# Output products in column tiles of 384 and 256 + 128 tokens, and two products of a unit in swapped order

## The chip, the cores and the metric

The kernel runs on one core of a Trainium2 chip. The metric is the device time of one launch in microseconds (us); lower is better. Before the change the median of three runs was 2621.24 us (2618.13 to 2623.8).

## What is computed

All in fp32: a causal convolution of seven taps (softmaxed per head, 8 heads) over 8 sequences of 4096 tokens with 192 features, and then on the 32768 tokens a feed-forward block with RMS norm and SwiGLU, width 1536.

```python
w = softmax(weight, axis=-1)                        # 8 heads x 7 taps
x = conv(x_pad, w)                                  # (8, 4096, 192) -> (32768, 192)
xn = x / sqrt(mean(x * x) + 1e-6) * rms_g
g, val = xn @ w_gate, xn @ w_val                    # 192 -> 1536
out = (silu(g) * val) @ w_out                       # 1536 -> 192
```

## The kernel before

**Tiling.** The tokens are worked off in 32 pairs; a pair is two groups (g = 0, 1) of T = 512 tokens. The first pair goes through a plain routine (lines 991 and 1031). The other 31 each go through one `Pair` object, and these are nearly the whole time. One such pair is 60 products and then 42 output steps, on the matmul engine in the order of `Pair.products`.

**Products (line 754).** The hidden layer is computed in four units. A unit makes six tiles of 128 hidden features by 512 tokens (three feature blocks for two token groups), once for the gate and once for the value. By a fast matrix scheme it needs 15 products in place of 18; the right-hand sides are sums of token tiles (`XSUM`, tile `xc`, made by VectorE and GpSimd), the left-hand sides sums of weight blocks (`WSUM`). Every product is two matmuls of 64 rows by 512 columns that run side by side: h = 0 (gate) on the lower half of the array's rows, h = 1 (value) on the upper half. `CHAIN` and `CHAINS` give their order as (unit, bank v, index of the product): (0, 4, 5) adds product 5 into the PSUM bank that stands for v = 4. The kernel before already swaps two products of unit 0, so its unit 0 begins (4,11), (1,4), (5,6), (4,9), (0,8), (4,5), (5,13), (1,10), (4,7), (0,3), (5,2), (2,1).

**Evacuations.** Between the products of one bank its value is copied or added up by ScalarE (A), VectorE (V) or GpSimd (G). `Unit.do` has the steps: `S41` copies bank 4 after its second product into a tile (line 706 on ScalarE, 710 on VectorE), `S42` the same after its third; `S00` copies bank 0; `C` adds bank 5 to the tile copied by `S40` (line 774); `D5` adds the tile of `S00` into bank 5 (line 770); `S51` copies bank 5 after that; `F2` copies bank 4 into a new bank 2; `R` makes a result (line 778). The second figure is h. A product that adds to a bank must wait until the copy of the bank's former value is done.

**Order of the other engines.** `ORDER` is a list written by hand. `p2` stands for two entries of the matmul stream, and each other word for one step: the engine's letter, the step, v, h and the unit; a trailing `-` means a step of the pair before. Engines run in order, so the list sets the order within each engine; between engines only waits on data count. Further steps of the list: `VT11`, `VT21` turn output banks by 32x32 transposes (line 899), `Vbc` is one small transpose for the norm (line 490) that waits for two copies on GpSimd (line 483), `Gmul` scales by the norm (line 498), `Dst0`, `Dst1` store an output group (line 957), `Dload` loads tokens (line 144), `Dplace` and `DfetA`, `DfetB` move normed tokens to device memory and back as tiles (lines 633, 659). All `D` steps are issued by SyncE, except a part of the last pair's stores by ScalarE.

**Output steps (line 884).** The output product is a seven-product scheme over token groups, pairs of feature blocks and the two halves of the 192 outputs: `OUTS` lists the forms, 42 steps in all. A step multiplies one tile of 128 features by 512 tokens with a weight block of three times 32 columns (m = 0, 1, 2). The array is used as four column tiles of 32 columns (i = 0 to 3), each with its own weights and its own stream of tokens, writing its own 32 partitions of the same PSUM bank, 384 columns in use. Before the change the step is eight matmuls: four of 256 tokens (m = 0 on tiles 0 and 1, m = 1 on tiles 2 and 3, each tile taking every other block of 32 tokens) and four of 128 tokens (m = 2, a quarter of the tokens each). In fp32 every matmul shows in the trace as two records (two passes), each with its own weight load.

Of the kernel before, what the change touches and what calls it, by code (L numbers as in the profile page):

```python
# [19 lines left out]
def kernel(  # L20
# [11 lines left out]
    P = nc.NUM_PARTITIONS  # L32
# [10 lines left out]
    T = 512  # L43
# [3 lines left out]
    HP = P // 2  # L47
    KP = D // HP
    Q = 32
    NQ = P // Q  # L50
# [7 lines left out]
    LOW, UPP = slice(0, HP), slice(HP, P)  # L58
# [29 lines left out]

    SPAN = 1509
    ORDER = (  # L90
        "p2 VT11- p2 AS40.1.0 AS40.0.0 p2 AF0.0.0 GX9- AF0.1.0 Dst0- p2 VC.1.0 Dload- GX4- p2",
        "Vbc- AS41.0.0 VS41.1.0 VC.0.0 p1 AS00.1.0 p1 Gmul- VT21- AS00.0.0 p2 AS42.0.0",
        "VS42.1.0 p2 VD5.0.0 p1 VD5.1.0 AS51.0.0 p1 Dst1- VR1.0.0 AS51.1.0 p2 VR1.1.0 AF2.0.0",
        "p2 AF2.1.0 VR0.0.0 Dplace- AG1.0.0 p1 VR0.1.0 p1 AF3.0.0 AF3.1.0 p2 VR2.0.0 AG0.0.0",
        "p1 VR2.1.0 p1 AS44.0.0 GM0.1.0 AS44.1.0 p2 VR3.0.0 AG2.0.0 GM1.1.0 p1 VR3.1.0 p1",
        "AS40.0.1 VR5.0.0 AS40.1.1 p2 AG4.0.0 VR5.1.0 AG5.0.0 p1 VM4.1.0 p1 AF0.0.1 VF0.1.1",
# [140 lines left out]
    def load_out(i):  # L237
# [28 lines left out]
        out=taps[:], in0=w_sb[:], in1=stat[:].to_broadcast([P, H, K]), op=ALU.subtract  # L266
# [7 lines left out]
        out=taps[:], in0=taps[:], in1=ssum[:].to_broadcast([P, H, K]), op=ALU.mult  # L274
# [153 lines left out]
    def part_tap(p, k, j):  # L428
# [4 lines left out]
        if k == 0:  # L433
            h = SIDE[j]
            acc[p, j] = h, pick(h, False)
# [11 lines left out]
        if k == K - 1:  # L447
            h, i = acc.pop((p, j))
            free[h].append(i)
            ended[p] = ended.get(p, 0) + 1  # L450
            if ended[p] == len(SIDE):
                x_sb.pop(p)
# [229 lines left out]
    def pick(h, full):  # L682

        i = next((i for i in free[h] if ((h, i) in whole) == full), free[h][0])
        free[h].remove(i)
        return i
# [5 lines left out]
    def put(at, do):  # L692
        heapq.heappush(line, (at, next(tick), do))
# [10 lines left out]
    def copy(eng, dst, src, s=1):  # L704
        if eng == "A":
            nc.scalar.activation(out=dst, in_=src, func=AF.Copy, scale=float(s))  # L706
        elif s < 0:
            nc.vector.tensor_scalar(out=dst, in0=src, scalar1=-1.0, scalar2=None, op0=ALU.mult)
        else:
            nc.vector.tensor_copy(out=dst, in_=src)  # L710
# [5 lines left out]
    CHAINS = [  # L716
        [(u, 4, 11)] + [(u - 1, 4, 0)] * (u > 0) + [(u, *c) for c in CHAIN] for u in range(NU)
    ]
    CHAINS[0][2:4] = CHAINS[0][3:1:-1]
    CHAINS[-1][-3:] = [(NU - 1, 4, 12), (NU - 1, 2, 1), (NU - 1, 3, 14), (NU - 1, 4, 0)]  # L720
    FORK = {0: (1, 1), 2: (4, 1), 3: (5, -1)}
    RESULT = {1: ("42", -1), 0: ("41", -1), 2: ("51", -1), 5: ("44", -1), 3: ("c", 1)}
# [83 lines left out]
    NM = D // (2 * Q)  # L806
# [13 lines left out]
    )  # L820
    HOME = {"X": 0, "Y": 1, "Z": 1}
    SIDE = (0, 1, 0)
    RIGHT = {1: B11, 2: B21, 3: B22, 4: T4, 5: T1, 6: T2, 7: T3}

    class Pair:
# [36 lines left out]
        def products(self):  # L862
            for u, v, i in itertools.chain(*CHAINS):
                for h in range(2):
                    self.units[u].product(h, v, i)
                    yield
            for form, b, lo, hi in OUTS:
                first = form in (1, 7)
                if first:
                    self.open(b, False)  # L870
                for k in range(lo, hi):
                    src, right = self.left(form, k), RIGHT[form][:, k]
                    fresh = first and k == 0
                    wide = src.rearrange("p (b q e) -> p q b e", q=2, e=Q)
                    slim = src.rearrange("p (b q e) -> p q b e", q=NQ, e=Q)
                    for i in range(NQ):
                        self.tile(b, i, 0, 2 * P, right[:, i // 2], wide[:, i % 2], fresh)
                    yield
                    for i in range(NQ):
                        self.tile(b, i, 2 * P, P, right[:, 2], slim[:, i], False)  # L880
                    yield

        def tile(self, b, i, at, n, left, cols, fresh):
# [30 lines left out]
        def do(self, eng, name):  # L914
            act, *at = name.split(".")
            p, n = self.p, NM * P
            if name in self.past:
                return
            self.past.add(name)
            if len(at) == 2:  # L920
                self.units[int(at[1])].do(eng, act, int(at[0]))
            elif at:
                self.sum(int(act[1]), int(at[0]), eng)
            elif act == "c1":
                self.open("Y", True)
                copy(eng, self.some("Y"), self.some("X"))
            elif act in ("s7", "c2"):
                t = self.tl[act] = tiles.pop(0)
                copy(eng, t[:, 0:n], self.some("Z" if act == "s7" else "X"))
            elif act in ("C22", "C21"):  # L930
                t = self.tl["s7" if act == "C22" else "c2"][:, 0:n]
                b = "X" if act == "C22" else "Z"
                nc.vector.tensor_tensor(out=t, in0=self.some(b), in1=t, op=ALU.add)
                if b == "Z":
                    self.close(b)
                    if p == PAIRS - 1:
                        for name in ("T22", "T21", "st1"):
                            if name not in self.past:
                                self.do(eng, name)
            elif act in ("T22", "T21"):  # L940
                t = self.tl.pop("s7" if act == "T22" else "c2")
                self.turn(t, 1, int(act[2]) - 1)
                tiles.append(t)
            elif act in ("T11", "T12"):
                b = "Y" if act == "T11" else "X"
                self.turn(self.bank(b), 0, int(act[2]) - 1)
                self.close(b)
            elif act in ("st0", "st1"):
                g = int(act[2])
                r = p * PT + g * T  # L950
                o = self.o_sb.pop(g)[:].rearrange("p a d -> p (a d)")
                o = o.rearrange("p (b d) -> p b d", d=HP)
                for c, rows, lo, hi in ((0, LOW, 0, 8), (1, UPP, 0, 8), (2, slice(0, P), 8, 12)):
                    n = T // (hi - lo)
                    to = out[r : r + T, c * HP : (c + 1) * HP].rearrange("(b p) d -> p b d", p=n)
                    q = nc.scalar if c == 1 and p == PAIRS - 1 else nc.sync
                    q.dma_start(out=to, in_=o[rows, lo:hi, :])
            else:
                self.ahead(eng, act)

# [16 lines left out]
    def plain(hts):  # L977


        groups = [(u, g, f) for u in range(NU) for g in (1, 0) for f in range(NF)]  # L980
        groups[0 : 2 * NF] = [(0, g, f) for f in range(NF) for g in (1, 0)]
        held = {}

        def products():
            for u, g, f in groups:
                if len(hts) <= u:
                    hts.append(big.tile([P, 2, NF, T], F32, name="ht"))
                bks = held[u, g, f] = [free[h].pop(0) for h in range(2)]
                for k in range(KP):
                    for h in range(2):  # L990
                        nc.tensor.matmul(  # L991
                            out=bank(h, bks[h])[:], lhsT=wf[u][HALF[h], k * NF + f, :],
                            rhs=xb[HALF[h], g, k, :], start=(k == 0), stop=(k == KP - 1),
                            skip_group_check=True,
                        )
                yield

        def silus():
            for i in groups:
                sg = tiles.pop(0)  # L1000
                nc.scalar.activation(out=sg[:], in_=bank(0, held[i][0])[:], func=AF.Silu)
                held[i].append(sg)
                yield

        def values():
            for u, g, f in groups:
                *bks, sg = held.pop((u, g, f))
                nc.vector.tensor_tensor(  # L1008
                    out=hts[u][:, g, f, :], in0=bank(1, bks[1])[:], in1=sg[:], op=ALU.mult
                )  # L1010
                tiles.append(sg)
                for h in range(2):
                    free[h].append(bks[h])
                yield

        return products(), silus(), values()

    LAG = 138
# [114 lines left out]
    p, sl, v = plain(hts)  # L1133
# [31 lines left out]
    c = base + 200  # L1165
# [4 lines left out]

    for j in range(len(SIDE)):
        put(c + 240 + 700 * (j // 2), functools.partial(part_tap, 2, 0, j))
        for k in range(1, K):
            at = c + 250 + 100 * k + 50 * j if j < 2 else c + 960 + 80 * k
# [58 lines left out]
```

## Time and profile before

The profiled execution took 2620.28 us, of which the span of the profile is 2618.4 us.

| Item | Value |
|---|---|
| median of 3 runs | 2621.24 us |
| profiled execution / its span | 2620.28 us / 2618.4 us |
| matmul records, weight loads | 29002 each |
| busy: VectorE / ScalarE / GpSimd | 2265.0 / 1617.3 / 2079.0 us |
| one pair, the commonest length | 79.5 us: 52.06 us of products, 27.44 us of output steps |
| first pair and set-up, to the first product of line 754 | 136.76 us |

A pair's length is the distance between the starts of the first product matmul (line 754) of one pair and of the next. In the page, PE is the matmul stream and PEld the weight loads beside it. A busy matmul engine need not be at its peak, since matmuls overlap: the distance between the starts of matmuls on the same tile says more than the length of one.

### The profile page before, as it was taken

To read this page: it belongs to the slowest core of one execution; us is meant where nothing else is said; L and a number is where in the kernel's file an instruction comes from. 1 tells how busy PE (TensorE), PEld (TensorE's weight loads), DVE (VectorE), ACT (ScalarE), POOL (GpSimd) and SP (SyncE) were. 2 spreads that over 40 slices of the span, in tenths; PEclk is the share of its full clock that TensorE was granted. 3 is DMA by queue.
4 is the path that set the end of the run, shared out by engine and by line. 5 is a ranking of instruction groups with operands and counts; after the bars stand their busy time and mean duration, and the time that the engine had idled before them with its cause. 6 is when DMAs were issued, how large, how long until landed. Compare 5 with 4: busy or idle time off the path is not lost.

```text
span 2618.4 us, 71028 instructions
## 1 busy us (share of the span) xinstructions
PE 2580.3 (99%) x29002; PEld 1866.1 (71%) x29002; DVE 2265.0 (87%) x3617; ACT 1617.3 (62%) x2967; POOL 2079.0 (79%) x1693
## 2 busy tenths in 40 slices
PE   6999999999999999999999999999999999999999
PEld 3677777777767777777776777777777777777776
DVE  8888888888888988888888888888898888888875
ACT  5375556765556765557755567655577555676554
POOL 3877788877888777888787887778887778877776
PEclk9999999999999999999999999999999999999999
DMA  6322331323312223213233222233132332222210
GB/s 143 54 47 51 63 53 36 63 39 63 63 36 53 50 51 63 54 35 63 39 63 63 41 48 51 51 63 58 34 59 44 58 63 43 46 57 45 50 38 14
DMA packets 510659, 138.01 MB, mean 53 GB/s; under 512 B 482300, under 2 KB 484860, under 8 KB 510205
## 3 DMA queue, kind: packets, MB, share of 16 engines
q1 hardware_dynamic: 508716, 133.18, 27.2%
q8 instruction: 227, 3.72, 0.6%
q14 instruction: 100, 0.82, 0.1%
q10 hardware_dynamic: 1616, 0.29, 0.1%
HBM read 83.87 MB, written 49.55 MB: 51 GB/s over the span
## 4 chain that ended last, share of the span: by engine, by line
PE 96%; DVE 2%; DMA 1%; issue 0%; POOL 0%; ACT 0%; SPq 0%; DVEq 0%; POOLq 0%; ACTq 0%
PE ps L754 62%; PE ps L884 33%; PE ps L991 1%; PE ps L1031 1%; DMA x<-in_x_dram 0%; DMA xb<-xd 0%; DVE y L405 0%; DVE ht L1008 0%; DVE y L420 0%; DVE y L393 0%; DVE xc L304 0%; PE ps L594 0%; DVE wf L319 0%; ACT xb L614 0%; DVE xc L668 0%
## 5 line engine op out<-in xcount | busy, mean ns | idle before, releaser
L754 PE MATMUL ps<-xc,wf 64*128 64x512 f32 x4960 | 1252.8, 592 | 1.6 <-DVE xc L668 1.1
L754 PEld LDWEIGHTS ps<-xc,wf 64*128 64x128 f32 x4960 | 760.9, 186 | 308.1 <-issue 88.8
L754 PE MATMUL ps<-xb,wf 64*128 64x512 f32 x2480 | 709.1, 589 | 0.0
L706 ACT ACTIVATE tls<-ps 128x512 f32<-128x512 f32 (+1 forms) x636 | 365.7, 589 | 375.5 <-PE ps L884 211.0
L798 POOL TENSOR_TENSOR ht<-ht,tile 128x512 f32<-128x512 f32 x295 | 375.2, 1279 | 272.8 <-ACT tile L791 271.4
L706 ACT ACTIVATE tile<-ps 128x512 f32<-128x512 f32 x697 | 400.1, 594 | 271.2 <-PE ps L754 158.4
L754 PEld LDWEIGHTS ps<-xb,wf 64*128 64x128 f32 x2480 | 392.9, 187 | 141.2 <-issue 38.7
L706 ACT ACTIVATE ps<-ps 128x512 f32<-128x512 f32 (+1 forms) x651 | 366.9, 578 | 54.1 <-PE ps L884 38.9
L912 POOL TENSOR_TENSOR early<-ht 128x512 f32<-128x512 f32 x279 | 379.2, 1364 | 4.9
L444 DVE SCALAR_TENSOR_TENSOR ps<-xh,tp,ps 128x512 f32<-128x512 f32 x450 | 312.1, 745 | 1.7 <-ACT ps L436 0.6
L798 POOL TENSOR_TENSOR ht<-ht,tls 128x512 f32<-128x512 f32 x201 | 255.2, 1276 | 72.4 <-ACT tls L791 70.9
L884 PE MATMUL ps<-ht,wo_sb 128*32 128x256 f32 (+1 forms) x6944 | 310.5, 326 | 0.0
L778 DVE TENSOR_TENSOR tile<-ps,tile 128x512 f32<-128x512 f32 x373 | 255.0, 687 | 56.1 <-PE ps L754 53.5
L884 PEld LDWEIGHTS ps<-ht,wo_sb 128*32 128x32 f32 x6944 | 216.3, 110 | 92.8 <-POOL ht L798 23.5
L884 PE MATMUL ps<-ht,x 128*32 128x256 f32 (+1 forms) x5952 | 250.1, 326 | 0.4 <-issue 0.4
L912 POOL TENSOR_TENSOR ht<-ht 128x512 f32<-128x512 f32 x186 | 248.3, 1350 | 0.0
L791 ACT ACTIVATE tile<-tile 128x512 f32<-128x512 f32 x373 | 233.1, 629 | 12.3 <-DVE tile L778 12.3
L884 PEld LDWEIGHTS ps<-ht,x 128*32 128x32 f32 x5952 | 190.5, 110 | 54.2 <-issue 1.6
L778 DVE TENSOR_TENSOR ht<-ps,tls 128x512 f32<-128x512 f32 x311 | 211.8, 681 | 0.0
L778 DVE TENSOR_TENSOR ht<-ps,tile 128x512 f32<-128x512 f32 x309 | 210.4, 681 | 0.1
L778 DVE TENSOR_TENSOR tls<-ps,tls 128x512 f32<-128x512 f32 x247 | 169.4, 686 | 28.1 <-PE ps L754 26.1
L884 PE MATMUL ps<-early,x 128*32 128x256 f32 (+1 forms) x4464 | 193.5, 326 | 0.0
(129 smaller groups left out, 3132.8 us busy)
## 6 DMA issues: line engine op xcount, KB each, us to landing
xb<-xd SPq DMA_DIRECT2D x124, 384.0 KB
xd<-yn SPq DMA_DIRECT2D x248, 96.0 KB
out_dram<-o_sb SPq DMA_DIRECT2D x184, 128.0 KB
xh<-in_x_dram SPq DMA_DIRECT2D x192, 105.0 KB
xh<-in_x_dram SPq DMA_DIRECT2D x56, 98.4 KB
ht<-in_moe_w_gate_dram SPq DMA_DIRECT2D x12, 192.0 KB
ht<-in_moe_w_val_dram SPq DMA_DIRECT2D x12, 192.0 KB
tls<-in_moe_w_out_dram SPq DMA_DIRECT2D x8, 192.0 KB
```

Source lines behind the costliest of these rows:

```text
L444: nc.vector.scalar_tensor_tensor(out=dst, in0=xk, scalar=w, in1=at, op0=ALU.mult, op1=ALU.add)
L706: nc.scalar.activation(out=dst, in_=src, func=AF.Copy, scale=float(s))
L754: nc.tensor.matmul(out=self.new(v, h, True) if first else self.old(v, h), lhsT=wf[self.u][HALF[h], WAT[i], :], rhs=x_op(XOP[i])[HALF[h]], ...
L778: nc.vector.tensor_tensor(out=self.hv(v) if h else t[:], in0=self.old(v, h), in1=t[:], op=plus(s))
L791: nc.scalar.activation(out=t[:], in_=src[:], func=AF.Silu)
L798: engine[eng].tensor_tensor(out=self.hv(v), in0=src, in1=t[:], op=ALU.mult)
L884: nc.tensor.matmul(out=self.bank(b)[i * Q : (i + 1) * Q, at : at + n], lhsT=left, rhs=cols, start=fresh, stop=True, skip_group_check=True, ...
L912: engine[eng].tensor_tensor(out=dst, in0=a, in1=b, op=op)
L991: nc.tensor.matmul(out=bank(h, bks[h])[:], lhsT=wf[u][HALF[h], k * NF + f, :], rhs=xb[HALF[h], g, k, :], start=(k == 0), stop=(k == KP - 1 ...
L1031: nc.tensor.matmul(out=bank(h, bks[h])[:, w : w + D], lhsT=hts[f // NF][HALF[h], g, f % NF, j * P : (j + 1) * P], rhs=wo_sb[HALF[h], f, :] ...
```

## The change

The output step becomes six matmuls: m = 0 and m = 1 on tiles 0 and 1, each over the first 384 tokens; m = 2 on tiles 2 and 3, over 256 tokens each; then the last 128 tokens of m = 0 and m = 1 on tiles 2 and 3. Each tile still takes 384 columns in all. The generator yields after the first four and after the last two, so a step is still two entries of the stream.

The output rows lie differently in the bank, so a store of 512 tokens becomes five DMAs in place of three (32 x 12, 32 x 12, 64 x 8, 32 x 4 and 32 x 4 rows of 64 floats, in place of 64 x 8, 64 x 8 and 128 x 4); the bytes and the rows are the same. In the last pair ScalarE issues two of the five per store, in place of one of three.

In unit 0 the products (5,13) and (4,5) change places. In `ORDER` the step `Vbc-` goes ahead of both `VC` steps, `VC.0.0` ahead of `VS41.1.0`, `AS00.0.0` and `AS00.1.0` change places, `VD5.0.0` goes ahead of `AS42.0.0` and `VS42.1.0`, and `VD5.1.0` and `AS51.0.0` keep their place after `VS42.1.0`.

```diff
     ORDER = (
-        "p2 VT11- p2 AS40.1.0 AS40.0.0 p2 AF0.0.0 GX9- AF0.1.0 Dst0- p2 VC.1.0 Dload- GX4- p2",
-        "Vbc- AS41.0.0 VS41.1.0 VC.0.0 p1 AS00.1.0 p1 Gmul- VT21- AS00.0.0 p2 AS42.0.0",
-        "VS42.1.0 p2 VD5.0.0 p1 VD5.1.0 AS51.0.0 p1 Dst1- VR1.0.0 AS51.1.0 p2 VR1.1.0 AF2.0.0",
+        "p2 VT11- p2 AS40.1.0 AS40.0.0 p2 Vbc- AF0.0.0 GX9- AF0.1.0 Dst0- p2 VC.1.0 Dload- GX4- VC.0.0 p2",
+        "AS41.0.0 VS41.1.0 p1 AS00.0.0 p1 Gmul- VT21- AS00.1.0 p2 VD5.0.0 AS42.0.0",
+        "VS42.1.0 p2 VD5.1.0 AS51.0.0 p2 Dst1- VR1.0.0 AS51.1.0 p2 VR1.1.0 AF2.0.0",
...
     CHAINS[0][2:4] = CHAINS[0][3:1:-1]
+    CHAINS[0][5:7] = CHAINS[0][6:4:-1]
...
+    WIDE = NM * P
...
-                    wide = src.rearrange("p (b q e) -> p q b e", q=2, e=Q)
-                    slim = src.rearrange("p (b q e) -> p q b e", q=NQ, e=Q)
-                    for i in range(NQ):
-                        self.tile(b, i, 0, 2 * P, right[:, i // 2], wide[:, i % 2], fresh)
+                    two = src.rearrange("p (b q e) -> p q b e", q=2, e=Q)
+                    for i in range(2):
+                        self.tile(b, i, 0, WIDE, right[:, i], src[:, 0:WIDE], fresh)
+                    for i in range(2):
+                        self.tile(b, 2 + i, 0, T // 2, right[:, 2], two[:, i], fresh)
                     yield
-                    for i in range(NQ):
-                        self.tile(b, i, 2 * P, P, right[:, 2], slim[:, i], False)
+                    for i in range(2):
+                        self.tile(b, 2 + i, T // 2, T - WIDE, right[:, i], src[:, WIDE:T], False)
                     yield
...
-                for c, rows, lo, hi in ((0, LOW, 0, 8), (1, UPP, 0, 8), (2, slice(0, P), 8, 12)):
-                    n = T // (hi - lo)
-                    to = out[r : r + T, c * HP : (c + 1) * HP].rearrange("(b p) d -> p b d", p=n)
+                wide, half = WIDE // Q, T // HP
+                for c, i, m, lo, hi, at in (
+                    (0, 0, 1, 0, wide, 0), (1, 1, 1, 0, wide, 0), (2, 2, 2, 0, half, 0),
+                    (0, 2, 1, half, wide, WIDE), (1, 3, 1, half, wide, WIDE),
+                ):
+                    n = m * Q
+                    rows = slice(r + at, r + at + (hi - lo) * n)
+                    to = out[rows, c * HP : (c + 1) * HP].rearrange("(b p) d -> p b d", p=n)
                     q = nc.scalar if c == 1 and p == PAIRS - 1 else nc.sync
-                    q.dma_start(out=to, in_=o[rows, lo:hi, :])
+                    q.dma_start(out=to, in_=o[i * Q : i * Q + n, lo:hi, :])
```

## The prediction

> **What bounds the kernel now.** I read the page first, then the waits, the chain and the timeline of an ordinary pair, and at last the starts of single matmul records.
>
> ```profile
> PE 2580.3 (99%) x29002; PEld 1866.1 (71%) x29002; DVE 2265.0 (87%) x3617; ACT 1617.3 (62%) x2967; POOL 2079.0 (79%) x1693
> ...
> q8 instruction: 227, 3.72, 0.6%
> ...
> PE 96%; DVE 2%; DMA 1%; issue 0%; POOL 0%; ACT 0%; SPq 0%; DVEq 0%; POOLq 0%; ACTq 0%
> PE ps L754 62%; PE ps L884 33%; PE ps L991 1%; PE ps L1031 1%; DMA x<-in_x_dram 0%; DMA xb<-xd 0%; DVE y L405 0%; DVE ht L1008 0%; DVE y L420 0%; DVE y L393 0%; DVE xc L304 0%; PE ps L594 0%; DVE wf L319 0%; ACT xb L614 0%; DVE xc L668 0%
> ```
>
> The matmul stream is the end-setting chain: 62% products, 33% output steps. So an edit counts only by what it does to this stream's pace or gaps. The pace of the output steps, from the timeline:
>
> ```profile
> 1003.00 7.98 PE L884 MATMUL ps<-ht,x 128*32 128x256 f32 x192
> 1010.80 1.48 PE L884 MATMUL ps<-ht,wo_sb 128*32 128x256 f32 x32
> ```
>
> 192 records at 16 per step are 12 steps, in 1010.80 - 1003.00 = 7.80 us: 650 ns a step. On one column tile the records start 216, 216, 109 and 109 ns apart. Two equations (256 and 128 columns) give 0.83 ns a column and pass, and about 2.5 ns for each record. The gaps, from the waits of PE and of its weight loads, and from the chain:
>
> ```profile
> PE ps L884 <- issue: 3.3, 5, 1.4
> ```
>
> ```profile
> PEld ps L884 <- issue: 6.1, 9, 1.6
> ...
> PEld ps L754 <- POOL xc L668: 13.4, 17, 1.0
> ```
>
> ```profile
> 1068.90 13.33 PE ps L884 x321
> 1082.23 0.53 issue
> 1082.76 14.51 PE ps L884 x264
> ```
>
> "Issue" means that no data was late; these stops lie in the output steps only. The third view shows one. And the waits in unit 0, in the timeline of a pair that starts at 1176.69 us:
>
> ```profile
> 1180.47 0.69 DVE L710 COPY tls<-ps 128x512 f32<-128x512 f32 x1
> ...
> 1180.49 0.60 ACT L706 ACTIVATE tile<-ps 128x512 f32<-128x512 f32 x1 [0.56 <-PE ps L754]
> ...
> 1181.08 0.68 DVE L774 TENSOR_TENSOR tile<-ps,tile 128x512 f32<-128x512 f32 x1
> ...
> 1181.20 0.33 PEld L754 LDWEIGHTS ps<-xc,wf 64*128 64x128 f32 x4 [0.77 <-POOL xc L668]
> ```
>
> The load at 1181.20 is that of (4,5). It names GpSimd, but GpSimd was done earlier; the copies of bank 4 (lines 706 and 710, S41) end at 1181.09 and 1181.16, and they hold it.
>
> [...] in the output steps that begin at 430.67 us one tile falls 425 ns behind after a stop, and the others' 128-column records start before its earlier 256-column ones, at an unchanged 650 ns a step and at unchanged record lengths (379 and 273 ns). [...] I see 90 ns from the last product to the first output step. [...] 227 packets of 16,384 bytes are 58,112 instructions, PE's matmuls and loads being 58,004.
>
> **Part 1, fewer records.** A step has 12 records and 12 loads for 16 and 16. It is not faster for it: tiles 2 and 3 still run 256, 256, 128 and 128 columns, 650 ns; tiles 0 and 1 run 384 twice, 2 x (320 + 2.5) = 645 ns, and wait for nothing but cannot end the step. Value taken: 0. That tiles of unequal length don't hold each other up is argued from the skewed stretch; the trace has no unequal step. Bounds: 42 x 31 = 1302 steps by -10 ns (the pure columns) = -13 us, and by +24 ns (a late load lengthened records there from 379 to 403) = +31 us.
>
> **Part 2, instruction blocks.** PE eats 32 instructions in 650 ns, 20.3 ns each; afterwards 24, 27.1 ns each. Following q8 against PE's position: a block is asked for when 0.69 of the former is eaten; PE stops when the new one has not landed by 1.54 to 1.66, about 0.97 x 256 = 248 instructions or 5.0 us later. Landing takes 1.7 us in the median, but behind the xb transfers 5.0 to 6.1 us five times, and those are exactly the long stops. Adding what each pair's output steps lost to them (pairs 4, 5, 12, 18, 19, 23 to 26: 0.56, 1.11, 0.93, 0.99, 0.82, 0.29, 0.25, 0.18, 1.97) gives 7.1 us. Afterwards there are 248 x 27.1 = 6.7 us, more than the worst landing. I take -6.8, keeping 0.3 for a worse phase; bounds 0 and -7.1.
>
> **Part 3, unit 0.** Times in us from the pair's first product; half h = 1 ends the products, so it counts. Before: 104 ns at the first product (stays), at (4,5) 141 + 105 = 246 ns, at (2,1) 116 ns, together 466. The 105 is a load that could not be hidden: the first record takes 693 instead of 589 ns.
> After: (5,13) is due at 4.40 and needs both C. VectorE: Vbc (0.24) moves to the idle time 1.38 to 2.92, its GpSimd copies being done at 1.61; C.1 2.99 to 3.68; C.0 3.60 to 4.28. Semaphore to load took 42 ns here, the second half's load follows 36 ns later: 4.37, lag 36 ns before the matmul, so about 105 - 36 = 69 ns lost. S41.1 now ends at 4.89; (4,5), due at 5.3, doesn't wait. But S42 now has one product of cover, (1,10), where it had two. (4,5) ends at 6.186; semaphore 0.18, copy 6.39 to 7.08 (0.692; VectorE is free, D5.0 ends at 6.26), load at 7.136, matmul due at 7.044: 93 + 104 = 197 ns lost at (4,7). So the old wait returns three products later. Behind it: D5.1 6.99 to 7.68, R1.0 to 8.26, R1.1 to 8.87 (9.08 before), F2.1 to 9.5; (2,1) is due at 9.81, so its 116 go. After: 104 + 69 + 197 = 370; gain 96 ns, x 30 pairs (the first waits for other things) = -2.9 us. Bounds: both new waits vanish, 362 x 30 = -10.9; nothing gained, 0.
>
> **Part 4, stores.** Two more DMAs per store on SyncE. Its cost per issue and its slack:
>
> ```profile
> 1188.38 2.02 SPq L957 DMA_DIRECT2D out_dram<-o_sb  x3
> 1190.50 5.25 SPq L633 DMA_DIRECT2D xd<-yn  x8
> 1228.70 1.29 SPq L659 DMA_DIRECT2D xb<-xd  x2
> ```
>
> 0.66 us each, four more a pair: loads (line 144) 1.3 us later, the xd writes 2.6 us later. SyncE idles from 1195.75 to 1228.70, and the loads' first readers (ScalarE, from 1228.7) come 40 us after them: cost 0. Without that cover the fetches, and the sums behind them, would be 2.6 us late. At the end nothing covers: each queue issues one more, up to 0.6 us, but the last is a quarter of the former's rows and data landed from 2614.6 to 2617.2 at a steady rate: +0.2 taken, bounds 0 and +0.6.
>
> **Sum.** -6.8 - 2.9 + 0.2 = -9.5 against the profiled execution's 2620.28 (span 2618.4 and 1.9 around it): 2610.8. The median of the runs is 1.0 above that execution: 2611.7.
>
> **Rivals.** (a) Stops stay: something other than instruction rate decides the landings. For: two stops lie at the same place of the output steps. Against: the five late landings match the five longest. 2611.7 + 6.8 = 2618.5. (b) Unit 0 runs free: 2611.7 - 8.0 = 2603.7. Against: the copy takes longer than the one product of cover. (c) The step falls to 640 ns: 2611.7 - 13.0 = 2598.7. Against: the 2.5 ns show alike with two tiles and with four, so they belong to the record. (d) Slower: on a tile of 384 columns a pending load keeps those of tiles 2 and 3 back, once a step. For: no unequal step in the trace[...]. Against: the skewed stretch. At 24 ns a step 2611.7 + 31.2 = 2642.9; it decides from 9.5 / 1302 = 7.3 ns a step.
>
> **Chances.** Forecast 0.66 (2606 to 2616.5), (a) 0.09, (b) 0.10, (c) 0.05, (d) 0.10. A measurement of this kernel can tell about 0.2%, 5.2 us, from no change: faster means below 2616.0. Faster 0.62 + 0.10 + 0.05 = 0.77; same 0.04 + 0.09 = 0.13; slower 0.10. The range 2602 to 2620 holds forecast, (a) and (b), 0.85.
>
> **What would show it.** Steps still 650 ns, no stop named "issue" in the output steps, q8 at about 186 packets; a wait at (4,7) on lines 706 and 710 and none at (2,1); ordinary pairs of 79.4 us. Steps of over 657 ns or records longer than their form would make it wrong.

## The result, and the profile after

The changed kernel takes 2610.36 us (median of 6 runs, 2609.71 to 2611.92), beside 2619.64 us for the kernel before (median of 6, 2617.59 to 2623.8). The ratio is 0.9962, 95% interval 0.9951 to 0.9973: faster by 0.38%. The forecast was 2611.7 us, reckoned from the first three runs of before at 2621.24. The profiled execution is one of 2609.93 us, its span 2607.8.

First the page after (busy times, queue q8 and the chain of the work that ended last):

```profile
span 2607.8 us, 60706 instructions
...
PE 2573.4 (99%) x23794; PEld 1874.5 (72%) x23794; DVE 2273.2 (87%) x3617; ACT 1618.3 (62%) x2967; POOL 2078.9 (80%) x1693
...
q8 instruction: 186, 3.05, 0.5%
...
PE 97%; DVE 2%; DMA 0%; issue 0%; ACT 0%; POOL 0%; SPq 0%; DVEq 0%; POOLq 0%; ACTq 0%
```

29002 - 23794 = 5208 matmul records are gone, 4 in each of 1302 output steps, and with them 41 of the 227 blocks of instructions. The bound is the same: the matmul stream. Its busy time fell by only 6.9 us, since a step with fewer, longer records takes as long as before. The waits of PE, all that the view lists:

```profile
PE ps L533 <- ACT early L401: 18.5, 2, 17.3
PE ps L594 <- ACT xc L587: 5.6, 1, 5.6
PE ps L1039 <- POOL wo_sb L311: 2.5, 2, 1.4
PE ps L999 <- ACT xb L614: 1.1, 1, 1.1
PE ps L999 <- DVE ht L1016: 0.5, 2, 0.2
PE ps L755 <- DVE xc L668: 0.3, 1, 0.3
PE ps L755 <- DVE o_sb L1051: 0.3, 1, 0.3
```

The line that named "issue" at the output steps is gone (they are line 887 now), here and among the weight loads. What is left lies in the set-up or is under half a microsecond. The chain of the twelfth pair, which before had a stop of 0.53 us in its output steps:

```profile
999.86 13.44 PE ps L887 x167
1013.30 51.98 PE ps L755 x240
1065.28 27.44 PE ps L887 x338
1092.71 17.49 PE ps L755 x79
```

27.44 us of output steps without a gap, exactly what an undisturbed pair took before: the step itself got no faster. The forms of its records (name, shape and count, then busy us and mean ns):

```profile
L887 PE MATMUL ps<-ht,wo_sb 128*32 128x384 f32 x1736 | 301.8, 487 | 0.0
L887 PE MATMUL ps<-ht,wo_sb 128*32 128x256 f32 x1736 | 261.7, 380 | 0.0
...
L887 PE MATMUL ps<-ht,wo_sb 128*32 128x128 f32 x1736 | 168.5, 273 | 0.0
```

487, 380 and 273 ns are one straight line, 107 ns for 128 columns more; 380 and 273 are the lengths of before, so tiles of unequal length don't lengthen each other's records. Read record by record, tiles 0 and 1 start a step every 645 ns and run ahead of tiles 2 and 3, which need 650. Unit 0 of a pair that starts at 1172.06 us (loads, and the copies that hold them):

```profile
1175.05 1.29 DVE L775 TENSOR_TENSOR tile<-ps,tile 128x512 f32<-128x512 f32 x2 [1.15 <-PE ps L755]
...
1176.39 0.30 PEld L755 LDWEIGHTS ps<-xc,wf 64*128 64x128 f32 x4 [0.60 <-DVE tile L775]
...
1178.41 0.60 ACT L706 ACTIVATE tile<-ps 128x512 f32<-128x512 f32 x1 [0.67 <-PE ps L755]
1178.45 0.69 DVE L710 COPY tls<-ps 128x512 f32<-128x512 f32 x1
...
1179.06 0.43 PEld L755 LDWEIGHTS ps<-xc,wf 64*128 64x128 f32 x4 [0.65 <-ACT tile L706]
```

The first line is both steps C in one go; the load of (5,13) follows at 1176.39 and costs 42 ns. The second group is the wait that came back: both copies S42 begin together, and the loads of (4,7) wait for them from 1179.06 on; (4,7) of half 1 loses 121 + 104 = 225 ns: it starts 121 ns late, and its first record is 104 ns longer.

Where the 10.6 us of span went, by the starts of matmuls (before, after):

| Stretch | before | after | difference |
|---|---|---|---|
| set-up and first pair | 136.76 | 136.66 | -0.1 |
| pair 1 of the 31 | 82.58 | 81.89 | -0.7 |
| pairs 2 to 30, ordinary length x 29 | 29 x 79.500 | 29 x 79.417 | -2.4 |
| pairs 2 to 30, what they took above that | 8.32 | 1.00 | -7.3 |
| last pair's first product to the end | 85.26 | 85.11 | -0.15 |

Of the 8.32, 7.1 were stops in output steps. Nothing in the change is known to act on the first two rows, and they vary by more without it: over all profiles here the first stretch lies between 135.9 and 137.0 us, and pair 1, leaving out the kernel of twelve matmuls below, between 81.9 and 84.4.

### The profile page after: what moved, and what is told of

Read it like the earlier page. It is cut to its first block, busy times and chain, and to the rows that moved or that the text cites. A ratio compares the mean times of both kernels' runs of the same rounds, so it can differ in the third digit from the quotient of the medians.

```text
span 2607.8 us, 60706 instructions
## 1 busy us (share of the span) xinstructions
PE 2573.4 (99%) x23794; PEld 1874.5 (72%) x23794; DVE 2273.2 (87%) x3617; ACT 1618.3 (62%) x2967; POOL 2078.9 (80%) x1693
## 4 chain that ended last, share of the span: by engine, by line
PE 97%; DVE 2%; DMA 0%; issue 0%; ACT 0%; POOL 0%; SPq 0%; DVEq 0%; POOLq 0%; ACTq 0%
PE ps L755 62%; PE ps L887 33%; PE ps L1039 1%; PE ps L999 1%; DMA x<-in_x_dram 0%; DVE y L405 0%; DVE ht L1016 0%; DVE y L420 0%; DVE y L393 0%; DVE xc L304 0%; DVE wf L319 0%; PE ps L594 0%; ACT xb L614 0%; DVE xc L314 0%; POOL wo_sb L311 0%
## 5 line engine op out<-in xcount | busy, mean ns | idle before, releaser
L706 ACT ACTIVATE tile<-ps 128x512 f32<-128x512 f32 (+1 forms) x677 | 390.9, 593 | 320.9 <-PE ps L755 189.6
L706 ACT ACTIVATE tls<-ps 128x512 f32<-128x512 f32 (+1 forms) x656 | 376.3, 590 | 315.0 <-PE ps L887 192.7
L887 PE MATMUL ps<-ht,wo_sb 128*32 128x128 f32 (+2 forms) x5208 | 318.6, 380 | 0.0
L887 PEld LDWEIGHTS ps<-ht,wo_sb 128*32 128x32 f32 x5208 | 234.4, 110 | 81.2 <-POOL ht L799 22.7
L887 PE MATMUL ps<-ht,x 128*32 128x128 f32 (+2 forms) x4464 | 250.7, 379 | 0.0
L887 PEld LDWEIGHTS ps<-ht,x 128*32 128x32 f32 x4464 | 184.7, 110 | 61.0
L779 DVE TENSOR_TENSOR ht<-ps,tile 128x512 f32<-128x512 f32 x322 | 219.3, 681 | 0.0
L779 DVE TENSOR_TENSOR ht<-ps,tls 128x512 f32<-128x512 f32 x298 | 202.9, 681 | 0.1
L887 PE MATMUL ps<-early,x 128*32 128x256 f32 (+2 forms) x3348 | 196.0, 379 | 0.0
```

The source lines that it names most:

```text
L779: nc.vector.tensor_tensor(out=self.hv(v) if h else t[:], in0=self.old(v, h), in1=t[:], op=plus(s))
L887: nc.tensor.matmul(out=self.bank(b)[i * Q : (i + 1) * Q, at : at + n], lhsT=left, rhs=cols, start=fresh, stop=True, skip_group_check=True, ...
```

## The experiments

Some words first. A block is 256 instructions of PE, one packet of queue q8 (16,384 bytes in the trace). The runs show the size: PE's recorded matmuls and loads come to 255.5 a packet before (58,004 over 227), 255.8 after (47,588 over 186) and 256.0 with the twelve matmuls below (78,836 over 308), and the stops come back at the same place of every 256. A stop is time that the output steps of a pair lose beyond their undisturbed length (27.44 us with eight and with six matmuls). A landing is counted as in the prediction, from the moment when PE has 0.69 of the former block behind it, taken as the request, to the end of the block's packet; the trace doesn't record the request itself, but after the set-up no packet of the kernel before starts earlier than 0.66, and the ten earliest lie between that and 0.70. The cover of a copy is the work that PE has to do between the product that the copy waits for and the product that waits for the copy.

The theory: most of the gain is that PE eats instructions more slowly and so no longer outruns the landing of their blocks; a small part is the new order in unit 0. The rivals were that the order carries the gain, that the layout does, and that the cover of a copy isn't what sets the waits. The first four kernels ran on one chip, with before at 2622.24 us; the last four on one, with before at 2620.52. Ratios are to these.

**The output steps alone.** The order and the list of before, everything else changed.

```diff
-        "p2 VT11- p2 AS40.1.0 AS40.0.0 p2 Vbc- AF0.0.0 GX9- AF0.1.0 Dst0- p2 VC.1.0 Dload- GX4- VC.0.0 p2",
+        "p2 VT11- p2 AS40.1.0 AS40.0.0 p2 AF0.0.0 GX9- AF0.1.0 Dst0- p2 VC.1.0 Dload- GX4- p2",
...
-    CHAINS[0][5:7] = CHAINS[0][6:4:-1]
```

> The changed kernel with the old order of the products and the old list, so only the output steps and their stores are new. Theory (the gain is mostly stops for instruction blocks, which fewer records remove): the stops of the output steps go, about -7 us, the stores cost +0.4 at the end, unit 0 keeps its 466 ns a pair: about 2613 where the kernel before has 2619.6. Rival (the new order carries the gain): within 2 us of the kernel before.

Measured 2612.37 us, ratio 0.9963 (0.9950 to 0.9975). Ordinary pairs 79.50 us, no stop in the output steps. Nearly the whole gain is in this part; the rival falls. No store cost shows at the end, where 0.4 us was expected: from the start of the last matmul to the end of the span are 5.81 us, 5.88 before.

**The order alone.** The output steps of before, the new order and list.

```diff
+    CHAINS[0][5:7] = CHAINS[0][6:4:-1]
```

> The kernel before with the new order of the products and the new list, the output steps as before. Theory: ordinary pairs fall from 79.50 to 79.42 us (wait at (5,13) about 42 ns, at (4,7) about 225, none at (2,1)), the stops for instruction blocks stay: about 2617, -2.5 us. Rival (the order carries the gain): about 2611.

Measured 2619.42 us, ratio 0.9990 (0.9983 to 0.9996). Ordinary pairs 79.42 us with the expected waits, 42 ns at (5,13) and 225 at (4,7), and the stops are there, more of them than in the profile of before (its waits of PE):

```profile
PE ps L885 <- issue: 6.9, 8, 1.6
```

By the starts they cost 11.3 us in this execution, against 7.1 in that of before. So the stops differ from execution to execution. By medians the two parts, 9.9 us for the output steps and 2.8 for the order, come to more than the 9.3 of the whole on its own chip; the difference is within the intervals.

**Eight matmuls in the new layout.** Each tile takes the same columns of the same tokens, but the two matmuls of 384 are cut into 256 and 128.

```diff
-                    for i in range(2):
-                        self.tile(b, i, 0, WIDE, right[:, i], src[:, 0:WIDE], fresh)
+                    for i in range(2):
+                        self.tile(b, i, 0, T // 2, right[:, i], src[:, 0 : T // 2], fresh)
...
+                    for i in range(2):
+                        self.tile(b, i, T // 2, P, right[:, i], src[:, T // 2 : WIDE], False)
```

> The changed kernel, but the two matmuls of 384 tokens cut into 256 and 128, so the step has eight matmuls again, with the new layout and the new order. Tells the number of records from the layout. Theory: a step stays at 650 ns (four records on every tile), stops named issue come back in the output steps, 4 to 8 us: about 2616 to 2618. Rival (the layout or the contiguous reads help): as the changed kernel, 2610.4.

Measured 2618.99 us, ratio 0.9989 (0.9982 to 0.9995), which is the ratio of the order alone. PE's waits have the stops again:

```profile
PE ps L889 <- issue: 2.1, 5, 0.8
```

By the starts 5.7 us in the profiled execution. The step is 650 ns. Layout, contiguous reads and five stores being those of the changed kernel, the number of records, each with its load, is what tells.

The traces of the three kernels with eight matmuls and all transfers (before, the order alone, this one) tie the stops to the blocks directly. Twenty gaps of over 0.3 us stand between matmuls of their output steps. Counted in PE's recorded instructions, all twenty begin at the same place of a block, 256 apart or a multiple of it (the six of before after the 193rd of 256, semaphore waits counted), and each ends 1.2 to 1.6 us after a block has landed. In none of the five kernels here with six matmuls does any pair have a stop.

**Without the transfers.** The kernel before with no fetch of xb from the third pair on; it leaves these loads out and computes with stale tokens.

```diff
         for rows in (LOW, UPP):
+            if p > 1:
+                continue
             nc.sync.dma_start(
```

> The kernel before without the transfers that fetch the token tiles xb from device memory from the third pair on, so it computes with stale tokens; everything else stays. Theory (blocks land late because they stand behind these transfers): the stops in the output steps go with the old eight matmuls, about -7 us, near 2612; landings of blocks stay under 3.5 us. Rival (PE simply eats blocks too fast for the fetch): the stops stay, about 2619.

Measured 2614.01 us, ratio 0.9969 (0.9957 to 0.9981). All eight matmuls are there, 227 blocks too, and PE's view names no issue at the output steps; of the weight loads' view one is left:

```profile
PEld ps L886 <- issue: 0.8, 1, 0.8
```

A landing in the output steps takes 1.4 us in the median and 2.2 at most, against 1.7 and 6.1 in before. The packet itself takes 1.5 us at most in both kernels: what the transfers lengthen is the time before it starts. So both are needed for a stop at eight matmuls: these transfers and the rate. Either one taken away removes it.

**Twelve matmuls.** Every step in pieces of 128 tokens.

```diff
+                    for c in range(0, T // 2, P):
+                        go = fresh and c == 0
+                        for i in range(2):
+                            self.tile(b, i, c, P, right[:, i], src[:, c : c + P], go)
+                        for i in range(2):
+                            self.tile(b, 2 + i, c, P, right[:, 2], two[:, i, c // Q : (c + P) // Q], go)
```

> The changed kernel with every output step cut into twelve matmuls of 128 tokens. PE then eats 48 instructions in a step, 13.6 ns each, so a block has 248 x 13.6 = 3.4 us to land. In the kernels with eight matmuls the landings beyond 3.4 us sum to 17 to 29 us over 163 blocks; with 245 blocks 25 to 43 us. Theory: steps of 655 ns (six records of 109 ns on a tile, +6.5 us in all) and 25 to 43 us of stops named issue: 2642 to 2660. Rival (stops come from the transfers, whatever the rate): 2610.4 + 6.5 + 7 = 2624.

Measured 2764.38 us, ratio 1.0550 (1.0534 to 1.0565): in the forecast direction, and far beyond its size. An undisturbed step takes 655 ns, as expected; nearly all the rest comes of stops (page and PE's waits):

```profile
q8 instruction: 308, 5.05, 0.8%
```

```profile
PE ps L891 <- issue: 98.3, 69, 3.3
```

By the starts the output steps of pairs 2 to 30 are 140 us longer than undisturbed. Some 16 us of it are not stops: eleven times, around the end of a stop of 2.5 to 3.6 us, the granted clock falls to 0.5 for 3.41 us (its mean is 0.992 in this execution, 0.997 to 0.999 in those of the other kernels), and records of 128 columns last 421 ns in place of 273. The landings beyond 3.4 us sum to 137 us, but that this is so near to 140 is chance. The longest landing without a stop is 2.6 us here, not 3.4; and a landing counted from PE's position contains the stop before it. With the earlier stop taken off, the landings beyond 2.5 us sum to 123 us, beside some 126 of stops over all pairs. What failed in the expectation was thus the limit, and to take the landings over from kernels that ask less often; here their median is 2.9 us and the longest 7.7. That each transfer now meets several blocks one after another may be part of the reason; it is not shown.

**The swap without the list.** The new order of the products, the old list for the other engines.

```diff
-        "p2 VT11- p2 AS40.1.0 AS40.0.0 p2 Vbc- AF0.0.0 GX9- AF0.1.0 Dst0- p2 VC.1.0 Dload- GX4- VC.0.0 p2",
-        "AS41.0.0 VS41.1.0 p1 AS00.0.0 p1 Gmul- VT21- AS00.1.0 p2 VD5.0.0 AS42.0.0",
+        "p2 VT11- p2 AS40.1.0 AS40.0.0 p2 AF0.0.0 GX9- AF0.1.0 Dst0- p2 VC.1.0 Dload- GX4- p2",
+        "Vbc- AS41.0.0 VS41.1.0 VC.0.0 p1 AS00.1.0 p1 Gmul- VT21- AS00.0.0 p2 AS42.0.0",
```

> The changed kernel with the new order of the products but the old list for the other engines, so VectorE adds C of half 0 after the copy of bank 4. Theory (the wait is set by when VectorE has read bank 5): C of half 0 ends at 5.07 us of the pair, its load follows 42 ns later, (5,13) is due at 4.40: 0.73 + 0.1 us lost there, (4,7) still loses 0.22: ordinary pairs of about 80.2 us, 2610.4 + 30 x 0.79 = 2634. Rival (the swap alone removes the wait): 2610 to 2611.

Measured 2648.71 us, ratio 1.0103 (1.0089 to 1.0117), slower than both kernels. The timeline of a pair that starts at 1188.08 us:

```profile
1191.86 0.69 DVE L710 COPY tls<-ps 128x512 f32<-128x512 f32 x1
1192.47 0.68 DVE L775 TENSOR_TENSOR tile<-ps,tile 128x512 f32<-128x512 f32 x1
...
1193.20 0.30 PEld L755 LDWEIGHTS ps<-xc,wf 64*128 64x128 f32 x4 [1.39 <-DVE tile L775]
```

VectorE works in the order of the list: C of half 0 stands behind the copy of 1191.86, starts at 1192.47, ends at 1193.15, and the load follows: 726 + 104 ns lost at (5,13), as worked out, and 225 at (4,7). Not foreseen were about 320 ns more in half 1 at (5,2) and (2,1) and 170 at the last one of the pair, probably because the evacuations behind stay late: 80.68 us a pair instead of 80.2, and 2648.7 us instead of 2634. The list is the half of this edit that makes it a gain.

**Two products of cover at (4,7).** (4,7) and (0,3) swapped as well, and one of the two copies of bank 4 for bank 2 moved to VectorE.

```diff
+    CHAINS[0][8:10] = CHAINS[0][9:7:-1]
...
-        "p2 AF2.1.0 VR0.0.0 Dplace- AG1.0.0 p1 VR0.1.0 p1 AF3.0.0 AF3.1.0 p2 VR2.0.0 AG0.0.0",
+        "p2 VF2.1.0 VR0.0.0 Dplace- AG1.0.0 p1 VR0.1.0 p1 AF3.0.0 AF3.1.0 p2 VR2.0.0 AG0.0.0",
```

> The changed kernel with (4,7) and (0,3) swapped too, so the copy of bank 4 before (4,7) has two products of cover, and the copy of bank 4 for half 1 of bank 2 moved from ScalarE to VectorE. Theory (a copy with one product of cover loses about 0.2 us, one with two loses nothing): the 225 ns at (4,7) go, about 190 ns come at (2,1), which now has one product of cover after (4,7): 79.38 us a pair, -1 us, 2609.4, hardly to be told from 2610.4. Rival (the copy's engine sets the loss, not the cover): the loss goes altogether, 2603.5.

Measured 2612.74 us, ratio 0.9967 (0.9955 to 0.9979). The wait at (4,7) is gone, the one at (2,1) is 142 + 104 = 246 ns in place of 190, and a third at (3,14), 145 ns, was not foreseen; on VectorE the results that free banks now stand behind the copy, which fits but was not tested. 79.57 us a pair, where 79.38 was expected.

**The same with both copies on ScalarE.**

```diff
+    CHAINS[0][8:10] = CHAINS[0][9:7:-1]
```

> As the last one, but both copies of bank 4 for bank 2 stay on ScalarE, one after the other. Theory: the second copy ends about 1.3 us after (4,7), with 0.86 us of cover, so half 1 of (2,1) loses about 0.58 us and (4,7) nothing: 79.77 us a pair, 2610.4 + 30 x 0.36 = 2621. Rival (the engine, not the cover): 2603.5 to 2610.

Measured 2618.22 us, ratio 0.9990 (0.9984 to 0.9997). Nothing lost at (4,7), 500 ns at (2,1) in half 1, 79.74 us a pair (79.77 expected). In both kernels the wait goes where the cover is shortest; the ordinary pairs of both are longer than the changed kernel's 79.42 us.

## Why the prediction was right

**Fewer records, step at 650 ns: right.** The undisturbed output steps take 27.24 us from first to last record before and after. Neither bound was drawn on: the records of tiles 2 and 3 kept the step at 650, and nothing was held back by the longer tiles. That tiles of unequal length don't hold each other up, which the prediction could argue only from a skewed stretch, is now shown for this case: they run past each other, by 5 ns a step (645 against 650). The 2.5 ns of a record are seen again: two, four and six records for the same 384 columns of a tile take 645, 650 and 655 ns.

**Instruction blocks, -6.8: right, and shown from both sides.** The stops went with fewer records, came back when only the number of records was restored, and went from the kernel before when only the transfers were taken out. Landings beside output steps are now 4.5 us at most, under the 6.7 allowed.

The allowance itself was reckoned too long. PE does not stop at 5.0 us in the kernel before: the landings beyond that sum to 1.3 us only, with 7.1 us of stops. In the three kernels with eight matmuls no landing of over 4.4 us goes without a stop, and a stop is as long as its landing less 4.2 us (4.1 to 4.4). Beyond 4.2 us the landings sum to 7.1, 11.7 and 5.4 us, where the stops are 7.1, 11.3 and 5.7. Of its own range, 1.54 to 1.66, the prediction took the upper end, where PE stood when the blocks behind the long stops landed; the limit is at the lower one, 1.54 - 0.69 = 0.85 of a block or 4.4 us. With twelve matmuls the limit is about 2.5 us at 13.6 ns an instruction; carried on in a straight line to 27.1 ns, the two limits give some 5.9 us for the changed kernel, which is an estimate. Its worst landing stays under that too, with less to spare.

That -6.8 fits so well is in part luck. It was read off one profiled execution, and others have 5.7 or 11.3 us of stops with eight matmuls. Going by the medians of the kernel with the new output steps alone (9.9 us below before), a usual run of before lost nearer to 10 us on that chip, by estimate.

**Unit 0, -2.9: right in place, close in size.** Ordinary pairs 79.417 us against 79.4 forecast. (5,13) loses 42 ns, not 69: the load of the second half follows 6 ns after the first, not 36. (4,7) loses 225, not 197: from the end of (4,5) through the copy to (4,7) it takes 0.98 us, not 0.95, while (4,5) ends 27 ns earlier than reckoned. These two misses cancel. (2,1) loses nothing in ordinary pairs (in the one whose timeline is shown, 60 ns); a wait of 11 ns in unit 1 is new. -83 ns a pair instead of -96, and -2.4 us over pairs 2 to 30.

**Stores, +0.2: not seen.** From the start of the last matmul to the end of the span are 5.88 us before and 5.82 after; the four other kernels with the new output steps and six matmuls have 5.71 to 5.81. SyncE ends its issuing 0.7 us later after the last matmul than before, and yet the last data land 0.36 us earlier; why, is open. In the pairs the stores are hidden, as argued; but 0.66 us per DMA was too much. SyncE's line of stores after:

```profile
1184.98 3.02 SPq L965 DMA_DIRECT2D out_dram<-o_sb  x5
1188.10 5.26 SPq L633 DMA_DIRECT2D xd<-yn  x8
```

Five in 3.02 us against three in 2.02, a good 1 us and not 1.3.

**What is not settled.** The waits of 0.2 to 0.35 us in the products of pairs 3, 5, 8 and 16 (some 1 us in all) are in both kernels or come and go between them; they weren't followed up.

## What to carry to other kernels

When a saturated engine shows gaps put down to issue and not to data, count the instructions in its queue: the length of the work on one block, at the pace of its densest stretch, against the time from request to landing. Leave a reserve; here PE stopped from 4.2 us on where a block was 5.2 us of work (256 at 20.3 ns). Fewer and longer instructions paid here although each step stayed at 650 ns (24 in place of 32, 9.9 us), and so should moving a bulk transfer out of that stretch, of which only leaving it out was tried (8.2 us). A copy that the next product on a bank waits for needed its own duration plus the way to and from it as cover: 0.98 us with a copy of 0.69, where one product gave 0.86. Swapping products moved the wait to whoever had the least cover next (from (4,7), 225 ns, to (2,1), 246 or 500 ns), and the lists of the other engines had to be reordered with it (without that 2648.71 us).

## What the runs showed of the hardware that was not expected

The time to issue a DMA differs with its shape, and not by the number of partitions alone: in the last store 32 partitions x 12 rows took SyncE 0.315 us and ScalarE 0.373, where 64 x 8 took 0.595 and 0.637 before; but 32 x 4 took SyncE 0.816. The stops don't grow in step with the rate: 24 instructions (records and loads) a step gave none, 32 gave 6 to 11 us, 48 some 126 us. And with 48 long stops cost twice: eleven of them, of about 2.5 us and more, each came with 3.41 us at half the granted clock, which no stop of the other kernels here did.
